# Attention into a mixture of experts on one core: gate columns beside v, merged routing steps, and a listed order

## The chip, the cores and the metric

The kernel runs on one NeuronCore of a Trainium2 chip. The core has five engines with queues of their own: TensorE (PE, with a second queue PEld for loading weights), VectorE (DVE), ScalarE (ACT), GpSimd (POOL) and SyncE (SP), and 16 DMA engines that move data between device memory and the on-chip SBUF. The metric is device microseconds (us) of one execution; shown are the median of several runs and the lowest and highest. Profiles are of one execution.

## The reference

Inputs are q, k and v of shape (8 batches, 8 heads, 576 positions, 64 channels) in float32 and three weight tables. The reference computes linear attention and then sends each token through one of eight experts:

```python
q_s = softmax(q, axis=-1)                 # over the 64 channels
k_s = softmax(k, axis=2)                  # over the 576 positions
kv  = einsum('bhsd,bhse->bhde', k_s, v)
x   = einsum('bhsd,bhde->bhse', q_s, kv)  # then (4608 tokens, 512)
logits = x @ w_gate                       # 8 experts
e      = argmax(logits)                   # one expert per token
y      = relu(x @ w1[e]) @ w2[e]          # 512 -> 1024 -> 512
out    = softmax(logits)[e] * y
```

Every softmax divides by its sum plus 1e-9.

## The kernel before, in words

The work has three parts. **Attention and routing**, one batch after another. SyncE loads k, q and v of a batch (`load`: steps LK, LQ, LV). VectorE takes the maximum of k (KM0, KM1; lines 321 to 325), TensorE turns it round (KM2, KM4), VectorE subtracts it (KS, line 357), ScalarE takes the exponential (KE), and TensorE sums k_s times v into `kv` (KV, line 375), whose first column collects the sum of k_s. ScalarE divides it into `kx` (N2), beside which the product of kv with the gate weights is put (G0 to G3). For q, VectorE finds the maximum (QM, line 441) and GpSimd subtracts it (QS, line 446). Each tile of 128 tokens is then turned round (TR), taken through ScalarE (EX), and multiplied with `kx` (MM, lines 500 and 503): 146 columns for each pair of heads, namely 128 of x, 2 sums and 16 of gate logits. VectorE adds epsilon to the sums (DE, line 508), inverts them (RE, 511), and in EV multiplies the logits into `lh` (line 515) and x into the token row `xr` (line 517). There are 36 such tiles: 4 in an even batch, 5 in an odd one.

Routing (`route`, nine times) sums the logits over the heads (LS, line 547), finds the expert of each token, counts tokens of each expert on TensorE (R5), and makes the row number in a sorted table `xs` in device memory; many small VectorE steps do this (lines 551 to 605). GpSimd then writes the token rows to `xs` with an indirect DMA for each tile (PU, line 613).

**The first expert step.** Once the first CUT batches are routed, the first 384 rows of expert 0 are loaded from `xs` (IL, line 692), turned round on TensorE (IT) and split in a high and a low part. The weights w1 of expert 0 are loaded in eight pieces through the tile `xt` (WG, line 654) and split by ScalarE (WH) and GpSimd (WL, line 662); w2 by ScalarE and VectorE (VH; VL, line 671), after the key and query tiles have given up their room (step SW). Layer 1 runs over eight blocks of the hidden width (L1, line 712, three products of four matmuls for each), then layer 2 for 128 rows (L4, line 726). A table of what the loop is to do is made from the final counts (T0 to T8), and SyncE writes rows of padding behind each expert's rows (PD, line 819).

**The expert loop** (`experts`). Each engine runs its own loop with semaphores between them. A step takes up to 384 rows of one expert. TensorE does layer 1 over 192, 256 or 384 columns (line 971), depending on how many rows the step has, and layer 2 for one, two or three tiles of 128 rows (line 987). VectorE turns the next rows round in blocks of 32 (line 1105). Ahead of the loop, TensorE finishes layer 2 of the first step (line 1013) and turns the rows of the first loop step round (line 1027).

The order of the first two parts is made by a planner: each step has an estimated cost and a due time, and `Plan.emit` puts the steps out as their turn comes. Engines work strictly in that order, and so does SyncE's queue of DMA issues. Extra matmuls into unused space (`fill`, `warm`) keep TensorE busy at places that a table names.

Of the kernel before, what the change touches and what calls it, by code (L numbers as in the profile page):

```python
# [8 lines left out]
F32 = mybir.dt.float32  # L9
# [9 lines left out]
WSTEP = 0.15  # L19
CUT = 5  # L20
# [21 lines left out]
WINDOW = 0.0
FILL = {('KM2', 1, 0): 5, ('KM2', 2, 0): 8, ('G0', 1, 0): 4, ('G0', 3, 0): 6, ('MM', 3, 2): 3, ('MM', 5, 0): 4, ('KM4', 7, 0): 8, ('G0', 6, 0): 3, ('IT', 4, 2): 4}
# [4 lines left out]
class Plan:  # L48

    LAG = {SP: 1.8, PE: 0.2, DVE: 0.2, ACTE: 0.2, POOL: 0.2}
    ISSUE, PUT, PUT_LAG = 1.4, 0.75, 1.2

    def __init__(self, bufs):
        self.bufs, self.steps = bufs, {}

    def add(self, name, b, i, eng, fn, after=(), take=None, until=(), part=1.0, at=0.0):
        self.steps[name, b, i] = SimpleNamespace(key=(name, b, i), eng=eng, fn=fn, after=[a for a in after], take=take, until=list(until),
                                                 us=COST[name] * part, rank=b + WHEN[name] + 0.02 * i, at=at)  # L60

    def start(self, a, x):
        if a.key[0] == "PU":
            return a.done
        if a.eng == x.eng:
            return a.end - a.us if x.eng == SP else a.end + 0.1 if x.eng == DVE else a.end
        return a.end + self.LAG[a.eng]

    def emit(self):
        todo = dict(self.steps)  # L70
        for x in todo.values():
            x.after = [self.steps[a] for a in x.after if a in self.steps]
            x.until = [self.steps[a] for a in x.until]
            x.end = None
        free = dict.fromkeys(self.LAG, 0.0)
        dma = 0.0
        taken = {t: [] for t in self.bufs}
        line = sorted((x for x in todo.values() if x.eng == SP), key=lambda x: x.rank)
        wait = list(todo.values())
        ready = []  # L80
        while wait or ready:
            rest = []
            for x in wait:
                (rest if any(a.end is None for a in x.after) else ready).append(x)
            wait = rest
            best = []
            for x in ready:
                if x.eng == SP and x is not line[0]:
                    continue
                t = max([free[x.eng], x.at] + [self.start(a, x) for a in x.after])  # L90
                if x.take and len(taken[x.take]) >= self.bufs[x.take]:
                    old = taken[x.take][-self.bufs[x.take]].until
                    if any(a.end is None for a in old):
                        continue
                    t = max([t] + [self.start(a, x) for a in old])
                best.append((t, x.rank, x))
            t0, _, first = min(best, key=lambda y: y[:2])
            t, _, x = min((y for y in best if y[2].eng == first.eng and y[0] <= t0 + WINDOW), key=lambda y: y[1])
            if x.eng == SP:
                line.pop(0)  # L100
                free[SP] = t
                dma = x.end = max(dma, t + self.ISSUE) + x.us
            else:
                free[x.eng] = x.end = t + x.us
            if x.key[0] == "PU":
                dma = max(dma, x.end + self.PUT_LAG) + self.PUT
                x.done = dma + self.LAG[SP]
# [7 lines left out]
def attention_moe(ctx: ExitStack, tc: tile.TileContext, q, k, v, w_gate, w1, w2, xs, out):  # L115
# [41 lines left out]
    xa_pool = xa.__enter__()  # L157
    ka = tc.tile_pool(name="ka", bufs=2, side="right")
# [103 lines left out]
    def consts():  # L262
# [8 lines left out]
        for i in range(2):  # L271
            nc.gpsimd.memset(XR[i][:, :, DM:], 0.0)
# [1011 lines left out]
```

## Time and profile before

| | |
|---|---|
| median of 3 runs | 621.72 us (615.68 to 622.42) |
| profiled execution | 612.61 us, of which 610.7 us are the span of the trace |
| PE busy | 576.1 us, 94% of the span |
| DVE busy | 328.7 us, 54% |
| ACT busy | 239.3 us, 39% |
| POOL busy | 131.6 us, 22% |
| DMA | 86.19 MB |

The span divides into three parts: attention and routing up to about 164 us, the first expert step and the passage to the loop up to 204 us, and the loop up to 605 us. A busy engine is not an engine at its peak, so the shares are read stretch by stretch.

### The profile page before, as it was taken

To read this page: it belongs to the slowest core of one execution; us is meant where nothing else is said; L and a number is where in the kernel's file an instruction comes from. 1 tells how busy PE (TensorE), PEld (TensorE's weight loads), DVE (VectorE), ACT (ScalarE), POOL (GpSimd) and SP (SyncE) were. 2 spreads that over 40 slices of the span, in tenths; PEclk is the share of its full clock that TensorE was granted. 3 is DMA by queue.
4 is the path that set the end of the run, shared out by engine and by line. 5 is a ranking of instruction groups with operands and counts; after the bars stand their busy time and mean duration, and the time that the engine had idled before them with its cause. 6 is when DMAs were issued, how large, how long until landed. Compare 5 with 4: busy or idle time off the path is not lost.

```text
span 610.7 us, 11400 instructions
## 1 busy us (share of the span) xinstructions
PE 576.1 (94%) x3811; PEld 508.0 (83%) x3812; DVE 328.7 (54%) x683; ACT 239.3 (39%) x495; POOL 131.6 (22%) x210
## 2 busy tenths in 40 slices
PE   6788968979998999999999999999999999999996
PEld 3477857767896999989898989898989999898995
DVE  6788989978870241627041413245706552662466
ACT  2557536646521221524121222225515342542453
POOL 3122555667451001020101010011010201101020
PEclk8999989989999999999999999999999999999999
DMA  9999998884754912080703020304170634145000
GB/s 256 285 263 243 304 309 228 236 249 158 261 216 143 304 30 74 0 241 8 216 17 87 17 55 31 70 34 124 72 224 17 201 122 119 52 146 178 28 21 5
DMA packets 85307, 86.19 MB, mean 141 GB/s; under 512 B 21023, under 2 KB 70687, under 8 KB 84640
## 3 DMA queue, kind: packets, MB, share of 16 engines
q1 hardware_dynamic: 79280, 66.82, 40.3%
q0 software_dynamic: 6000, 19.03, 8.4%
q8 instruction: 15, 0.25, 0.2%
q14 instruction: 12, 0.10, 0.1%
HBM read 63.88 MB, written 22.74 MB: 142 GB/s over the span
## 4 chain that ended last, share of the span: by engine, by line
PE 78%; DVE 7%; DMA 4%; issue 3%; SPq 2%; ACT 2%; POOL 2%; POOLq 0%; DVEq 0%; ACTq 0%
PE py L987 32%; PE pt L971 25%; PE ph L971 8%; PE ph L712 3%; DMA kt<-in_k 2%; PE kv L375 2%; PE xp L500 2%; DVE kp L321 1%; DVE qm L441 1%; DMA xs<-xr,posi 1%; POOL qs L446 1%; PE py L726 1%; PE py L1013 1%; ACT kx L393 1%; PE qT L487 1%
## 5 line engine op out<-in xcount | busy, mean ns | idle before, releaser
L987 PE MATMUL py<-w2h,hid 128*128 128x512 f32 x576 | 179.9, 390 | 0.0
L1117 DVE SCALAR_TENSOR_TENSOR hid<-pt,hid 128x384 fp32r<-128x384 f32 x84 | 46.4, 557 | 215.9 <-ACT hid L1052 215.6
L987 PEld LDWEIGHTS py<-w2h,hid 128*128 128x128 f32 x576 | 108.1, 188 | 22.2 <-issue 0.3
L1166 POOL DMA_INDIRECT out<-yt,ix x39 | 43.2, 1109 | 323.3 <-ACT yt L1043 323.3
L987 PE MATMUL py<-w2l,hid 128*128 128x512 f32 x288 | 112.1, 389 | 0.0
L1043 ACT ACTIVATE yt<-py,ga 128x512 f32<-128x512 f32 x39 | 26.8, 688 | 149.7 <-PE py L987 134.0
L1052 ACT ACTIVATE hid<-pt 128x384 fp32r<-128x384 f32 x84 | 41.3, 492 | 96.6 <-PE pt L971 91.5
L971 PE MATMUL pt<-xh,w1h 128*128 128x384 f32 (+2 forms) x336 | 64.9, 314 | 0.2 <-issue 0.2
L971 PE MATMUL pt<-xh,w1l 128*128 128x384 f32 (+2 forms) x336 | 64.8, 314 | 0.0
L971 PE MATMUL pt<-xl,w1h 128*128 128x384 f32 (+2 forms) x336 | 64.8, 314 | 0.0
L987 PEld LDWEIGHTS py<-w2l,hid 128*128 128x128 f32 x288 | 54.1, 188 | 10.7
L971 PEld LDWEIGHTS pt<-xh,w1h 128*128 128x128 f32 x336 | 54.7, 189 | 1.7 <-issue 0.6
L971 PEld LDWEIGHTS pt<-xl,w1h 128*128 128x128 f32 x336 | 54.3, 189 | 0.0
L971 PEld LDWEIGHTS pt<-xh,w1l 128*128 128x128 f32 x336 | 54.3, 189 | 0.0
L613 POOL DMA_INDIRECT xs<-xr,posi x36 | 36.9, 1024 | 45.7 <-DVE lh L515 23.4
L1105 DVE STREAM_TRANSPOSE xrow<-xt 128x1536 f32<-128x1536 f32 x14 | 41.3, 2951 | 3.6 <-DMA gx<-xs 3.6
L500 PE MATMUL xp<-kx,qTs 128*128 128x146 f32 x256 | 37.9, 295 | 2.9 <-DVE xr L517 1.5
L500 PEld LDWEIGHTS xp<-kx,qTs 128*128 128x128 f32 x256 | 33.9, 193 | 5.1 <-DVE xr L517 2.5
L446 POOL TENSOR_TENSOR qs<-qt,qm 128x1024 f32<-128x1024 f32 (+1 forms) x16 | 23.8, 1511 | 41.7 <-DVE qm L441 35.0
L492 ACT ACTIVATE qTs<-qT 128x512 f32<-128x512 f32 x36 | 21.2, 596 | 26.9 <-PE xp L500 15.4
L375 PE MATMUL kv<-vt,kt 128*64 128x65 f32 (+1 forms) x640 | 30.0, 236 | 0.4 <-DMA vt<-in_v 0.4
L1110 DVE TENSOR_TENSOR xl<-xrow,xh 128x1536 fp32r<-128x1536 f32 x14 | 24.6, 1757 | 10.1 <-ACT xh L1048 10.1
(207 smaller groups left out, 809.6 us busy)
## 6 DMA issues: line engine op xcount, KB each, us to landing
raw<-in_moe_w SPq DMA_DIRECT2D x10, 2048.0 KB, 8.8
vt<-in_v SPq DMA_DIRECT2D x16, 512.0 KB, 9.1
qt<-in_q SPq DMA_DIRECT2D x8, 1024.0 KB, 7.4
kt<-in_k SPq DMA_DIRECT2D x7, 1024.0 KB, 8.7
xt<-xs SPq DMA_DIRECT2D x32, 192.0 KB, 5.1
xs<-zr SPq DMA_DIRECT2D x11, 260.0 KB, 2.4
xt<-in_moe_w SPq DMA_DIRECT2D x8, 256.0 KB, 5.5
raw<-in_moe_w SPq DMA_DIRECT2D x4, 512.0 KB, 6.1
```

The costliest lines, as they stand in the source:

```text
L375: nc.tensor.matmul(o.kv[i * D:(i + 1) * D, c, lo:lo + D + 1], o.kt[:r, 2 * c + i, j, :], VT[b % 2][:r, 2 * c + i, at:at + D + 1], start=Fa ...
L446: nc.gpsimd.tensor_tensor(o.qs[:, j0:j1].rearrange("p j h d -> p h j d"), o.qt[:, :, j0:j1, :], o.qm[:, :, j0:j1, None].to_broadcast([P, H ...
L500: nc.tensor.matmul(xv[:, c, :KW], o.qT[i][:, c, :], kx[:, c, :], start=True, stop=True)
L613: s = nc.gpsimd.indirect_dma_start(out=xs, out_offset=bass.IndirectOffsetOnAxis(ap=n.pi[:, t - t0:t - t0 + 1], axis=0), in_=xr[:, t, :], i ...
L971: m = e.matmul(ph, wt[:, c, f * P:(f + 1) * P], xt[:, c, :w], start=(n == 0), stop=(n == 3 * NC - 1))
L987: m = e.matmul(g.PY[u], ht[:, f, u * P:(u + 1) * P], wt[:, f, :], start=(n == 0), stop=(n == 3 * NF - 1))
L1043: m = e.activation(g.YT[u], g.PY[u], AF.Copy, scale=g.GA[:, u:u + 1]).wait_op(sPY[u], cu[u], GE)
L1052: e.activation(g.HH[:, f, :], g.PH[f][:, :W], AF.Relu).wait_op(sPH[f], it, GE).then_inc(sHH[f], 1)
L1105: e.transpose(g.XR.rearrange("p c (k j) -> p k c j", j=32), xblocks(g.XT).rearrange("p k (l c) -> p k c l", c=NC)).wait_op(sX, ld, GE).the ...
L1110: e.tensor_tensor(v(g.XL), src, v(g.XH).bitcast(F32), op=ALU.subtract).wait_op(sXH, it, GE).then_inc(sXL, 1)
L1117: e.scalar_tensor_tensor(g.HL[:, f, :], g.PH[f][:, :W], 0.0, g.HH[:, f, :].bitcast(F32), op0=ALU.max, op1=ALU.subtract).wait_op(sHH[f], it ...
L1166: e.indirect_dma_start(out=g.out, out_offset=bass.IndirectOffsetOnAxis(ap=g.IX[:, u:u + 1], axis=0), in_=g.YT[u], in_offset=None, bounds_c ...
```

## The change

- **Columns of `kx`.** A pair of heads has its 146 columns as 8 gate, 64 x, 64 x, 8 gate, then the 2 sums. One VectorE multiply then writes x and logits together into the token row, which grows from 520 to 584 floats, and LS reads the logits out of that row.
- **Merged steps.** Epsilon is put into `kv` by the matmul that clears it; the running count is a column of the one-hot tile; the expert's base row is added on TensorE; epsilon of the gate softmax is a constant column; the last sum writes the integer position itself. Five kinds of small VectorE steps go.
- **Order.** The planner's costs are replaced by a list of all steps, each with its number of fills. The q tile has two buffers. Expert 0's w1 comes in two loads into a tile of its own, and the first expert step's rows come from the first 4 batches instead of 5.
- **First loop step.** Its rows are loaded in blocks and turned round by VectorE as in every other step, and SyncE reads the two table entries for that load before the loop's code starts.
- **Narrow layer 1.** The narrow form has 224 columns instead of 192, and the threshold for taking it is raised to 224 rows.

```diff
-CUT = 5
+CUT = 4
-COST = dict(VG=1.5, VH=1.0, VL=1.2, LK=3.3, LV=4.0, LQ=3.3, CD=1.1, CS=1.31, KM0=2.2, KM1=0.7, KM2=0.45, KM3=0.6, KM4=0.95,
...
+ORDER = """
+CD.0.0.0 LK.0.0.0 LK.0.1.0 LK.0.2.0 LK.1.0.0 KM0.0.0.0 LK.1.1.0 LQ.0.0.0 LV.0.0.0 KM0.0.1.0 KM1.0.0.0 KM2.0.0.47 KM3.0.0.0
...
-                o.qt = ka_pool.tile([P, H, FULL, D], F32, name="qt", bufs=1)
+                o.qt = ka_pool.tile([P, H, FULL, D], F32, name="qt", bufs=2)
...
-            nc.tensor.matmul(t, none16[:1].to_broadcast([1, P]), none16[:1, :, None].to_broadcast([1, NP, D + 2]), **flags)
+            nc.tensor.matmul(t, ones16[:65], eps16[:65], **flags)
...
-            TS(ks, ks, EPS, None, op0=ALU.add)
             nc.vector.reciprocal(o.kr, ks)
...
         def ev(i):
             xv, qd = o.xp[i], o.qd[i]
-            TT(o.lh[:, i].rearrange("p (c i) e -> p c i e", i=2), xv[:, :, 2 * D + 2:KW].rearrange("p c (i e) -> p c i e", i=2),
-               qd[:, :, :, None].to_broadcast([P, NP, 2, E]), op=ALU.mult)
-            TT(xr[:, i, :DM].rearrange("p (c i d) -> p c i d", c=NP, i=2), xv[:, :, :2 * D].rearrange("p c (i d) -> p c i d", i=2),
-               qd[:, :, :, None].to_broadcast([P, NP, 2, D]), op=ALU.mult)
+            TT(xr[:, i, :XW].rearrange("p (c i d) -> p c i d", c=NP, i=2), xv[:, :, :KG].rearrange("p c (i d) -> p c i d", i=2),
+               qd[:, :, :, None].to_broadcast([P, NP, 2, D + E]), op=ALU.mult)
...
         def lsum():
-            RED(lg, o.lh[:, sl].rearrange("p t h e -> p t e h"), op=ALU.add, axis=AX.X)
+            g = xr[:, sl, :XW].rearrange("p t (c x e) -> p t e c x", c=NP, e=E)[:, :, :, :, 0:KG // E:KG // E - 1]
+            RED(lg, g, op=ALU.add, axis=AX.XY)
...
-        def a7():
-            acc[b, t1] = cst.tile([P, E], BF, name=f"acc{b}_{t1}", tag="acc", bufs=3)
-            TT(acc[b, t1], acc[prev], sm, op=ALU.add)
-        def a8():
-            n.cm = small("cm")
-            TS(n.cm[:, :T], cm, float(-RS), float(E * RS), op0=ALU.mult, op1=ALU.add)
-        def a12():
-            TS(se, se, EPS, None, op0=ALU.add)
-        def a13():
-            TT(n.pi[:, :T], pos, n.cm[:, :T], op=ALU.add)
...
+    def w1_get(g):
+        f = slice(g * FW, (g + 1) * FW)
+        nc.sync.dma_start(I0.RAW1[:, :, f], w1[0].rearrange("(p c) f -> p c f", c=NC)[:, :, f])
...
-                    layer1(P + P // 2)
+                    layer1(2 * P - P // 4)
...
-        e.wait_ge(sX, 3 * 16)
-        for u in (2, 1, 0):
-            for c in range(NC):
-                m = e.transpose(g.PT[:, u, c, :], xcol(g.XT, u, c, DM), g.ident)
-        m.then_inc(sT, 1)
         first(2)
...
-        evac(lambda t: t.rearrange("p c (u t) -> p u c t", t=P), g.PT, g.XT[:, :, DM:DM + 2])
+        turn_x()
+        evac()
...
-        n = x.get(KD, 0, 0, 6)
-        row = x.get(ROW, 0, 0, E * RS)
-        for u in range(3):
-            with e.If(n > 2 * u):
-                e.dma_start(g.XT[:, u, :], g.xs[bass.ds(row + u * P, P), :]).then_inc(sX, 16)
+        rows(*g.AT0)
```

The list moves instructions at three places that matter below. First, the start of SyncE's queue. Before (`kt`, `vt`, `qt` are the key, value and query tiles, `in_` the inputs):

```order
L190 DMA kt<-in_k 128x4x256 x2
L192 DMA kt<-in_k 64x8x64
L190 DMA kt<-in_k 128x8x256
L192 DMA kt<-in_k 64x8x64
L196 DMA vt_90<-in_v 128x8x128 [waits Pool_49]
L204 DMA qt<-in_q 128x8x256
```

Now (`wg` are the gate weights, `zr` a tile of padding that GpSimd fills):

```order
L308 DMA wg<-in_moe_w_gate 64x4x8 [waits Pool_49]
L308 DMA wg<-in_moe_w_gate 64x4x8
L311 DMA xs<-zr 128x584 [waits Pool_49]
L311 DMA xs<-zr 128x584 x2
L206 DMA kt<-in_k 128x4x256 x2
L208 DMA kt<-in_k 64x8x64
```

The gate weights and the three writes of padding, which came ninth and later, now stand ahead of the first key load, and wait for GpSimd.

Second, GpSimd's queue at the split of expert 0's w1 (`w1l` is the low part of w1, `xs<-xr` the write of a tile of token rows, `xr_119` and `xr_120` the rows of an even and of an odd batch). Before, with the sixth batch's query rows `qs` ahead:

```order
L446 TENSOR_TENSOR qs<-qt,qm 128x512
L455 TENSOR_TENSOR qsr<-qr,qmr 128x512
L662 TENSOR_TENSOR w1l_62<-xt,w1h_61 128x512 x3
L609 COPY xr_115<-tok 128x5
L612 MEMSET spacer 1x1
L613 DMA xs<-xr_115,posi 42624x520
L662 TENSOR_TENSOR w1l_62<-xt,w1h_61 128x512 x2
```

Now:

```order
L667 TENSOR_TENSOR w1l_62<-raw_73,w1h_61 128x512 x3
L619 COPY xr_119<-tok 128x4
L667 TENSOR_TENSOR w1l_62<-raw_73,w1h_61 128x512
L622 MEMSET spacer 1x1
L623 DMA xs<-xr_119,posi 43776x584
```

The split stood among the writes of the fourth and fifth batches; now it stands behind the writes of the sixth, four pieces ahead of the seventh batch's four writes and four ahead of the eighth's.

Third, TensorE at the end of layer 1 of the first step (`ph` is a layer-1 block, `xp` the last token tile, `cn` the final count from which the table and the padding rows are made). Before, the last token tiles ran ahead of all of layer 1, and five blocks came behind the count:

```order
L712 MATMUL ph_2315<-xh,w1l_62 128x384 x4
L758 LDWEIGHTS ones_107
L758 MATMUL cn<-acc_5_2344,ones_107 128x8
L712 MATMUL ph_2352<-xh,w1h_61 128x384 x4
L712 MATMUL ph_2352<-xl,w1h_61 128x384 x4
```

Now:

```order
L521 MATMUL xp<-kx_99,qTs 128x146 x4
L713 MATMUL ph_2246<-xh,w1h_61 128x384 x4
L713 MATMUL ph_2246<-xl,w1h_61 128x384 x4
L713 MATMUL ph_2246<-xh,w1l_62 128x384 x4
L713 MATMUL ph_2271<-xh,w1h_61 128x384 x4
L713 MATMUL ph_2271<-xl,w1h_61 128x384 x4
L713 MATMUL ph_2271<-xh,w1l_62 128x384 x4
L759 LDWEIGHTS ones_109
L759 MATMUL cn<-oh_138,ones_109 128x8
L713 MATMUL ph_2295<-xh,w1h_61 128x384 x4
```

Four blocks of layer 1 stand ahead of the last token tile, and two blocks behind the count.

## Rows read from the trace of the kernel before

**Rows 1.** Windows by stage: length, busy (instructions) per engine, granted clock, DMA share, GB/s
```profile
0.00:44.00 44.00, 34.30 (x307) 22.95 (x308) 31.04 (x67) 19.50 (x48) 12.49 (x51) 0.96 1.07 266
44.00:107.00 63.00, 52.35 (x559) 43.93 (x559) 57.15 (x163) 36.60 (x107) 28.09 (x39) 0.95 1.03 272
107.00:164.00 57.00, 50.85 (x550) 42.27 (x546) 49.91 (x163) 33.60 (x88) 36.13 (x53) 0.97 0.75 232
164.00:182.00 18.00, 17.92 (x108) 16.81 (x109) 15.02 (x70) 6.50 (x12) 9.04 (x16) 1.00 0.52 198
182.00:204.00 22.00, 19.68 (x91) 15.47 (x91) 3.00 (x9) 3.94 (x5) 1.99 (x2) 1.00 0.59 207
204.00:605.00 401.00, 400.96 (x2207) 366.52 (x2205) 172.56 (x214) 138.44 (x236) 42.89 (x50) 1.00 0.30 90
```

**Rows 2.** Timeline of SyncE's queue: start us, duration us, line and operation
```profile
0.78 1.01 SPq L190 DMA_DIRECT2D kt<-in_k  x2
...
143.75 1.30 SPq L692 DMA_DIRECT2D xt<-xs  x3
...
173.44 9.08 SPq L819 DMA_DIRECT2D xs<-zr  x8
190.73 2.03 SPq L1241 DMA_DIRECT2D xt<-xs  x3
```

**Rows 3.** Timeline of GpSimd: the padding tile, and a write of token rows
```profile
6.12 0.14 POOL L140 IOTA zr<- 128x1 f32 x1
...
151.43 0.97 POOL L613 DMA_INDIRECT xs<-xr,posi  x1 [0.23 <-issue]
```

**Rows 4.** Timeline of VectorE: two small routing steps, a tile's multiplies
```profile
74.23 0.16 DVE L586 TENSOR_SCALAR cm<-own 128x5 f32<-128x5 f32 x1
74.35 0.17 DVE L599 TENSOR_SCALAR own<-own 128x5 f32<-128x5 f32 x1
...
151.40 0.22 DVE L515 TENSOR_TENSOR lh<-xp,qden 128x64 f32<-128x64 f32 x1
151.54 0.68 DVE L517 TENSOR_TENSOR xr<-xp,qden 128x512 f32<-128x512 f32 x1
```

**Rows 5.** Timeline of VectorE: two long instructions, and the first when undisturbed
```profile
81.16 3.98 DVE L321 TENSOR_TENSOR kp<-kt 128x512 f32<-128x512 f32 x1
...
85.63 0.69 DVE L321 TENSOR_TENSOR kp<-kt 128x512 f32<-128x512 f32 x1
...
116.65 2.93 DVE L322 TENSOR_TENSOR km<-kp 128x256 f32<-128x256 f32 x1
```

**Rows 6.** Timeline of GpSimd beside the first of these
```profile
81.64 2.93 POOL L446 TENSOR_TENSOR qs<-qt,qm 128x1024 f32<-128x1024 f32 x2
```

**Rows 7.** Groups by line and form: count, busy us, mean ns, idle before
```profile
L1105 DVE STREAM_TRANSPOSE xrow<-xt 128x1536 f32<-128x1536 f32 x14 | 41.3, 2951 | 3.6 <-DMA gx<-xs 3.6
L662 POOL TENSOR_TENSOR w1l<-xt,w1h 128x512 fp32r<-128x512 f32 x8 | 10.0, 1272 | 0.5 <-ACT w1h L658 0.4
L671 DVE TENSOR_TENSOR w2l<-raw,w2h 128x1024 fp32r<-128x1024 f32 x4 | 4.9, 1214 | 0.0
L547 DVE TENSOR_REDUCE own<-lh 128x32 f32<-128x256 f32 x4 | 2.4, 608 | 0.0
```

**Rows 8.** Chain that ended last, in order of time: start us, length us, engine, line
```profile
126.54 2.31 PE mb L176 x8
...
182.24 5.72 PE py L726 x24
...
196.15 1.72 PE pt L1027 x12
...
214.18 6.24 PE pt L971 x36
...
401.62 4.00 PE pt L971 x36
...
456.22 4.32 PE pt L971 x36
```

More of the change, by code (lines that the diff above doesn't have):

```diff
@@ L48 @@
 class Plan:
-    LAG = {SP: 1.8, PE: 0.2, DVE: 0.2, ACTE: 0.2, POOL: 0.2}
-    ISSUE, PUT, PUT_LAG = 1.4, 0.75, 1.2
     def __init__(self, bufs):
[L56 to L76, printed above, removed]
-        taken = {t: [] for t in self.bufs}
[L78 to L107, printed above, removed]
@@ new lines, in __init__, with add, emit @@
+        self.bufs, self.steps, self.fills = bufs, {}, {}
+    def add(self, name, b, i, eng, fn, after=(), take=None, until=()):
+        self.steps[name, b, i] = SimpleNamespace(eng=eng, fn=fn, after=list(after), take=take, until=list(until))
+    def emit(self, order):
+        queue = []
+        for word in order.split():
+            name, b, i, n = word.split(".")
+            key = (name, int(b), int(i))
+            queue.append(key)
+            self.fills[key] = int(n)
+        assert sorted(queue) == sorted(self.steps)
+        seen = set()
+        taken = {t: [] for t in self.bufs}
+        for key in queue:
+            x = self.steps[key]
+            assert all(a in seen for a in x.after if a in self.steps), key
@@ L108, in emit @@
             if x.take:
+                if len(taken[x.take]) >= self.bufs[x.take]:
+                    assert all(a in seen for a in taken[x.take][-self.bufs[x.take]].until), key
                 taken[x.take].append(x)
-            ready.remove(x)
+            seen.add(key)
             x.fn()
@@ L622, in route @@
         old = [("PU", b - 2, t) for t in range(t0, t1)]
[L623 removed]
+        add("LS", b, r, DVE, lsum, [("EV", b, t) for t in range(t0, t1)])
         add("R0", b, r, DVE, a0, [("LS", b, r)])
@@ L684, in first_count @@
         I0.cn = ps.tile([P, E], F32, name="cn", tag="sm", bufs=1)
-        nc.tensor.matmul(I0.cn, ones16, acc[last5], start=True, stop=True)
+        nc.tensor.matmul(I0.cn, ones16, OH[turn[last5]][:, 0], start=True, stop=True)
     def first_rows():
@@ L757, in t0 @@
             n.cn = ps.tile([P, E], F32, name="cn", tag="sm", bufs=1)
-            nc.tensor.matmul(n.cn, ones16, acc[B - 1, SLOT], start=True, stop=True)
+            nc.tensor.matmul(n.cn, ones16, OH[turn[B - 1, SLOT]][:, 0], start=True, stop=True)
         def t1():
@@ L877, in attention_moe @@
     tables()
-    for n in range(WARM):
-        add("WM", 0, n, PE, lambda n=n: warm(n), at=WARM0 + n * WARMD, take=None if n else "xp", until=[("WM", 0, WARM - 1)])
-    plan.emit()
+    plan.emit(ORDER)
     nc.gpsimd.memset(spacer, 0.0)
```

302 lines of the change are left out of this document (174 added, 128 removed).

## The prediction, made before the changed kernel ran

> **What bounds the kernel now.** I read the windows by stage first [rows 1]. In the loop, 204 to 605 us, TensorE is busy 400.96 of 401 us: there only a shorter or missing matmul helps. From 164 to 182 us TensorE is busy 17.92 of 18 us with the eight layer-1 blocks of the first expert step, 2.24 us each. Attention and routing, 0 to 164 us, have no such single owner. Up to 107 us the DMA share is above 1.0, so the loads queue behind each other; VectorE is busy 31.04 of the first 44 us, then 57.15 of 63 (91%) and 49.91 of 57 (88%). From 107 us the DMA share is 0.75. So the loads set the pace at the start, VectorE nearly sets it from 44 us, and what is left is 5.9 and 7.1 us in which VectorE waits, plus time in which it is held up while it counts as busy: one maximum over keys took 3.98 us, its like 0.69, and another instruction of that step 2.93 [rows 5].
>
> Last I read the chain [rows 8] for what the stages hand on: layer 2 of the first step (5.72 us), twelve transposes between it and the loop (1.72 us), and the loop's layer 1 by width.
>
> **The change part by part.**
>
> *The start.* The first key load is issued at 0.78 us [rows 2]. Behind the listed order it stands after three writes of the padding tile, whose last value GpSimd writes at 6.12 + 0.14 = 6.26 us [rows 3]. SyncE's queue is in order, so all key, value and query loads behind wait too, and with them everything. The bytes of the padding and the gate weights are moved today as well, only later in the same full queue; what is lost is the time with no load under way, 6.26 - 0.78 = **+5.5 us**. Ends: 0, if VectorE's slack of 13 us in the first 44 us swallows it, and +7, with the issue of the three writes. I take 5.5, because the DMA engines have no slack in that stage.
>
> *Fewer VectorE instructions.* The logits' multiply disappears 36 times; the next instruction starts 0.14 us after it [rows 4], so it is worth 5.0 us. The multiply into the token row grows from 512 to 576 elements: 0.68 us x 64/512 = 0.085, 36 times, 3.1 us back. Five kinds of small steps go: epsilon of kv 8 times, the running count, the base row, epsilon of the gate softmax and the last add 9 times each, 44 in all, at one step per 0.12 us [rows 4]: 5.3 us. Together -7.2 us. VectorE is 90% busy where they stand, so I count nine tenths, **-6.5 us**. Ends: -7.2, and 0 if the loads set the pace throughout. The sum of logits now reads a strided row; four tiles take 0.608 us today [rows 7], nine such sums 5.5 us; that they double is the far end, that they stay the same is what I take, since today's read is strided already. The new additive matmuls on TensorE lie beside VectorE's work.
>
> *The waits.* The list places one wait after another differently, and no row shows the result. Nothing back is one end. The other is all 13 us of VectorE's waits from 44 to 164 us and the 3.3 + 2.5 us of the held-up instructions, -19. Some of it must go: the eight fills ahead of the last batch's subtraction, 2.31 us on the chain [rows 8], are not in the list, w1's eight loads no longer stand between key, value and query loads, and a second q tile lets a load go out a batch earlier. But a wait that goes often uncovers the next. I take a quarter, **-5 us**.
>
> *Token rows* grow by 256 bytes: 4608 x 256 = 1.2 MB, 4.3 us of DMA at 272 GB/s [rows 1]. At a share of 0.75 from 107 us on this is covered; uncovered it costs those 4.3.
>
> *First expert step and passage.* The twelve transposes leave TensorE (1.72), and VectorE's turning takes 2.95 us [rows 7] while TensorE has the third tile of layer 2 to do, some 5.7 us. SyncE has the two table entries in hand, and its three row loads (2.03 us) become five. Against that, the final count now stands two blocks from the end of layer 1 instead of five. Behind the count, SyncE issues the eight padding writes for 9.08 us [rows 2]; TensorE has 2 x 2.24 + 5.72 = 10.2 us left, and the passage waits for the writes to land. Today they are issued by 182.5 and layer 2 ends at 188.0, which leaves 5.4 us. So up to 2 us are gained and up to 2.5 lost: **0**.
>
> *Narrow layer 1.* Thirty-six matmuls take 6.24 us at 384 columns, 4.32 at 256, 4.00 at 192 [rows 8]: 0.173, 0.120, 0.111 us each. From 384 to 256 that is 0.42 ns for each column; the same line gives 0.107 at 224 and 0.093 at 192, but 192 shows 0.111, so a floor is reached before, and 224 should cost that floor. The reference's inputs leave two last steps of 211 and 194 rows, which go from 256 to 224, and three of 158, 173 and 34, which go from 192 to 224. Each step has 96 such matmuls: 2 x 96 x 0.009 = **-1.7 us**; on a straight line between 192 and 256 it would be +0.4.
>
> Sum: 5.5 - 6.5 - 5 + 0 - 1.7 = -7.7. The profiled execution took 612.61 us (a span of 610.7), 1.5% less than the median of 621.72; it would come to 604.9. The same 7.7 us off the median give 614.0, and I predict **614 us**.
>
> **The rivals.**
>
> *No change: the loads set the pace.* For it: the DMA share above 1.0 to 107 us [rows 1]. Then what VectorE saves turns into waiting, and the start's 5.5 us and the wider rows of the first four batches (18 tiles, 0.6 MB, 2.2 us) stand against w1's 2.1 MB, which no longer run ahead of the last loads (7.7 us at 272 GB/s): 0, and with the loop's -1.7, 620. Against it: VectorE at 91% while the queue is full.
>
> *Slower: GpSimd's queue in the end of attention.* The first step's rows are read behind the last value load, then w1 is loaded, and GpSimd must do nine writes, four low parts, four writes and four low parts before the fifth layer-1 block may start. A write takes 0.09 + 0.97 + 0.23, some 1.28 us with its pause [rows 3], a low part 1.27 [rows 7]: 13 x 1.28 + 8 x 1.27 = 26.8 us. Four blocks add 9.0 us. Layer 2 starts at 182.2 today, so the rows must land by 146.4 us; today they are issued at 143.75 [rows 2]. With the start 5.5 us later they could land at 153, and layer 2 starts at 188.8: +6.6, with 2.5 from the padding and -1.7 from the loop +7.4, 629. It decides from a landing at 146.4 us on, and costs over 1% from 152. Against it: the read no longer waits for the fifth batch's writes, which held it today.
>
> *VectorE and GpSimd hold each other up at the end.* The 3.98 us began while GpSimd was at the query subtraction, which read SBUF from 81.64 for 2.93 us [rows 5, 6]; VectorE's instruction has both its inputs in SBUF and ended at 85.14, 0.6 us after that one. The low parts of w1 stand now beside the four low parts of w2 on VectorE, 1.21 us each [rows 7], of the same kind, in a stretch where VectorE is busy 15.02 of 18 us. If each is held for one low part of w1, 4 x 1.27 = 5.1 us come back to VectorE, and to the hidden rows for which layer 1 waits: -2.6, 619. Against it: the list puts writes between the low parts, and a layer-1 block leaves 2.24 us for VectorE's 0.55. The Trainium skill, SBUF — State Buffer, "Who interferes with whom", says that a VectorE instruction with two SBUF inputs and a GpSimd instruction that reads SBUF take a shared read interface in turn, and that the later one is blocked for the whole of the other. The trace agrees, with the 3.98 us.
>
> *A denser order.* Half the waits go instead of a quarter: another -5, 609; at its best 604. For it: behind the third batch's keys the list has 17 fills where the planner's table had 32, as if it left TensorE fewer gaps.
>
> *The change doesn't do what it says*: the narrow form is not taken, or the wide multiply costs as much as the two. -1.7 or -1.9 are missing: 616.
>
> **How the numbers follow.** A difference of 1%, 6.2 us, is about what a measurement here can tell from none; the three runs shown lie 6.7 us apart. Chances: the forecast 0.45, of which 0.35 lies more than 1% below; denser order 0.12; no change 0.20; holding up 0.08; GpSimd's queue 0.13; not as said 0.02. Faster 0.35 + 0.12 = 0.47; the same 0.10 + 0.20 + 0.08 + 0.02 = 0.40; slower 0.13. The likeliest case alone, with the bounds of start, passage and waits, is 610 to 618. Nearly half the chance is on other cases: from 605, nearly the best of the denser order, to 625, which leaves out most of the slower case and no more.
>
> **What would show it.** In the changed profile: the first key load at 6.3 us or later; VectorE with some 7 us less work in front of layer 1 and no separate logits multiply; its waits between 44 us and layer 1 below 13 us; the first layer-2 block of the first step at about 175 us; no width of 192 or 256 in the loop but five of 224 at 4.0 us for 36 matmuls. I am wrong if the last batch's loads land when they do today and the rest only follows; if GpSimd is busy without a pause up to the fifth layer-1 block; or if the late start is made up within the first batches, which would make the gain larger by 5 us.

## The result: slower by 1.4%, and the profile after

The changed kernel takes 627.14 us (four runs, 625.18 to 628.25), the kernel before, beside it, 620.47 (615.68 to 622.42): a ratio of 1.0136, 95% interval 1.0087 to 1.0185. Forecast were 614 us (605 to 625) and a gain. The profiled execution took 627.72 us, of which 625.9 are its span.

The windows of the changed kernel by stage (length; busy us and instructions of TensorE, its weight loads, VectorE, ScalarE, GpSimd; granted clock, DMA share, GB/s), to be read against [rows 1]:

```profile
0.00:44.00 44.00, 34.23 (x219) 18.93 (x221) 25.82 (x56) 13.81 (x34) 10.82 (x53) 0.92 0.95 234
44.00:107.00 63.00, 54.34 (x612) 46.33 (x612) 52.74 (x132) 36.83 (x109) 27.74 (x39) 0.92 1.10 285
107.00:168.20 61.20, 55.83 (x586) 48.74 (x584) 46.06 (x134) 37.13 (x100) 29.78 (x47) 0.92 0.75 232
168.20:195.40 27.20, 21.78 (x119) 19.94 (x120) 21.88 (x65) 7.38 (x14) 12.59 (x20) 0.87 0.30 116
195.40:218.30 22.90, 17.22 (x79) 13.54 (x77) 5.99 (x13) 3.44 (x4) 4.48 (x7) 1.00 0.84 256
218.30:621.00 402.70, 401.89 (x2208) 367.13 (x2208) 172.51 (x215) 138.98 (x236) 43.12 (x50) 1.00 0.31 90
```

The loop is about as long as before (402.7 and 401 us). Layer 1 of the first expert step, 18 us with TensorE busy throughout, now lasts 27.2 with TensorE busy 21.78 at a granted clock of 0.87. VectorE is busy 124.6 us ahead of that stage and waits 43.6.

SyncE's queue (start, duration, line and operation), against [rows 2]: the first key load goes out at 7.74 us instead of 0.78, the first step's rows earlier than before, the padding writes 18 us later.

```profile
6.33 1.37 SPq L311 DMA_DIRECT2D xs<-zr  x3
7.74 1.39 SPq L206 DMA_DIRECT2D kt<-in_k  x2
...
130.49 1.47 SPq L690 DMA_DIRECT2D xt<-xs  x3
...
191.32 8.20 SPq L823 DMA_DIRECT2D xs<-zr  x8
...
206.51 0.40 SPq L914 DMA_DIRECT2D gx<-xs  x1
```

The groups by line and form (count, busy us, mean ns, idle before), against [rows 7]: the wide multiply, the loop's turning, and the low parts of w1 and w2. Those of w2 took 1.214 us each and take 2.589.

```profile
L1102 DVE STREAM_TRANSPOSE xrow<-xt 128x1536 f32<-128x1536 f32 x15 | 44.1, 2941 | 17.5 <-DMA gx<-xs 17.5
L536 DVE TENSOR_TENSOR xr<-xp,qden 128x576 f32<-128x576 f32 x36 | 27.1, 753 | 0.6
L676 DVE TENSOR_TENSOR w2l<-raw,w2h 128x1024 fp32r<-128x1024 f32 x4 | 10.3, 2589 | 0.0
L667 POOL TENSOR_TENSOR w1l<-raw,w1h 128x512 fp32r<-128x512 f32 x8 | 10.0, 1277 | 0.0
```

The mean hides that three of the four are as before and one is not. VectorE's timeline in layer 1 (start, duration):

```profile
172.05 0.55 DVE L720 SCALAR_TENSOR_TENSOR hid<-ph,hid 128x384 fp32r<-128x384 f32 x1
172.52 6.70 DVE L676 TENSOR_TENSOR w2l<-raw,w2h 128x1024 fp32r<-128x1024 f32 x1
...
179.23 0.54 DVE L720 SCALAR_TENSOR_TENSOR hid<-ph,hid 128x384 fp32r<-128x384 f32 x1
```

GpSimd's there:

```profile
172.05 0.97 POOL L623 DMA_INDIRECT xs<-xr,posi  x1 [0.23 <-issue]
173.05 3.75 POOL L667 TENSOR_TENSOR w1l<-raw,w1h 128x512 fp32r<-128x512 f32 x3
176.74 0.18 POOL L619 COPY xr<-tok 128x3 f32<-128x3 f32 x1
176.88 1.25 POOL L667 TENSOR_TENSOR w1l<-raw,w1h 128x512 fp32r<-128x512 f32 x1
```

And TensorE's, with two windows around it:

```profile
174.15 0.86 PE L713 MATMUL ph<-xh,w1l 128*128 128x384 f32 x4
179.83 1.65 PE L713 MATMUL ph<-xh,w1h 128*128 128x384 f32 x4 [4.82 <-DVE hid L720]
181.28 1.48 PE L713 MATMUL ph<-xl,w1h 128*128 128x384 f32 x4
```

```profile
175.00:180.00 5.00, 0.18 (x2) 0.17 (x2) 5.00 (x4) 0.49 (x1) 3.17 (x5) 0.80 0.00 0
180.00:185.00 5.00, 5.00 (x22) 4.69 (x23) 2.57 (x9) 0.49 (x1) 0.00 (x0) 0.52 0.01 3
```

One low part of w2 lasts 6.70 us: from 0.53 us before GpSimd's row of low parts to 1.09 us after its end. The hidden rows `hid` (line 720) stand behind it in VectorE's order, TensorE waits 4.82 us for them, and then runs some 5 us at 0.52, its lower clock of 1.2 GHz: four matmuls take 1.48 us that took 0.86.

The chain of waits (start, length), against [rows 8]: a wait for extra matmuls at the start, the slow block, the last piece of the first loop rows, their turning, and layer 1 at 384 and at 224 columns.

```profile
28.06 3.66 PE mb L191 x9
...
179.83 4.21 PE ph L713 x12
...
206.51 5.49 DMA gx<-xs
212.03 2.92 DVE xrow L1102
```

```profile
218.30 8.08 PE pt L973 x36
...
418.27 4.01 PE pt L973 x36
422.28 2.68 PE ph L973 x24
424.96 4.02 PE pt L973 x36
```

**Chips.** The runs below came from several chips. On one of them the kernel before takes 620 us, on the three others 612 to 613; so only ratios to the kernel before beside it are compared. By its times the profile above is from the slower kind; that of [rows 1] was not shown to be. Executions of one kernel on one chip also differ in the granted clock: of ten of e8 below, four took 606.0 to 608.1 us at a mean of 0.988 to 0.991, six 612.6 to 614.1 at 0.973 to 0.977. Both kernels were profiled again on one chip, and these two profiles give the account. TensorE's rows of the kernel before (layer 1, layer 2, first loop step):

```profile
162.32 0.95 PE L712 MATMUL ph<-xh,w1h 128*128 128x384 f32 x4 [0.21 <-DVE pe L555]
180.41 0.50 PE L726 MATMUL py<-w2h,hid 128*128 128x512 f32 x1
```

```profile
201.88 6.50 PE pt L971 x36
```

Of the changed kernel:

```profile
156.85 0.94 PE L713 MATMUL ph<-xh,w1h 128*128 128x384 f32 x4 [0.18 <-DVE xr L536]
183.87 0.47 PE L727 MATMUL py<-w2h,hid 128*128 128x512 f32 x1
```

```profile
207.12 8.06 PE pt L973 x36
```

In us, from the start of the one row to the start of the next:

| stage | before | changed | difference |
|---|---|---|---|
| to layer 1 of the first step | 162.32 | 156.85 | -5.5 |
| layer 1 | 18.09 | 27.02 | +8.9 |
| layer 2 to the loop | 21.47 | 23.25 | +1.8 |
| first 36 matmuls of the loop | 6.50 | 8.06 | +1.6 |
| the rest of the loop | 400.7 | 399.6 | -1.1 |
| span | 609.1 | 614.8 | +5.7 |

### The profile page after: what moved, and what is told of

Its sections match the earlier page's. It is cut to its first block, busy times and chain, and to the rows that moved or that the text cites. A ratio compares the mean times of both kernels' runs of the same rounds, so it can differ in the third digit from the quotient of the medians.

```text
span 625.9 us, 11354 instructions
## 1 busy us (share of the span) xinstructions
PE 585.3 (94%) x3813; PEld 514.6 (82%) x3814; DVE 325.0 (52%) x610; ACT 237.6 (38%) x495; POOL 129.5 (21%) x213
## 4 chain that ended last, share of the span: by engine, by line
PE 77%; DVE 10%; issue 3%; ACT 3%; DMA 3%; SPq 2%; another core or an unknown queue 1%; POOL 1%; POOLq 0%; DVEq 0%; ACTq 0%
PE py L989 31%; PE pt L973 25%; PE ph L973 8%; PE xp L521 3%; PE kv L402 3%; DVE kt L383 2%; PE qT L508 1%; DVE xr L536 1%; PE ph L713 1%; DMA kt<-in_k 1%; DVE kp L347 1%; DMA gx<-xs 1%; ACT kx L419 1%; DVE qm L464 1%
## 5 line engine op out<-in xcount | busy, mean ns | idle before, releaser
L973 PE MATMUL pt<-xh,w1h 128*128 128x384 f32 (+1 forms) x336 | 65.0, 315 | 3.2 <-DVE xl L1107 3.2
L973 PE MATMUL pt<-xl,w1h 128*128 128x384 f32 (+1 forms) x336 | 65.0, 315 | 0.0
L973 PE MATMUL pt<-xh,w1l 128*128 128x384 f32 (+1 forms) x336 | 65.0, 315 | 0.0
L1102 DVE STREAM_TRANSPOSE xrow<-xt 128x1536 f32<-128x1536 f32 x15 | 44.1, 2941 | 17.5 <-DMA gx<-xs 17.5
L623 POOL DMA_INDIRECT xs<-xr,posi x36 | 35.6, 988 | 50.2 <-DVE kp L347 10.4
L521 PE MATMUL xp<-kx,qTs 128*128 128x146 f32 x256 | 40.7, 308 | 0.4 <-DVE ge L579 0.3
L521 PEld LDWEIGHTS xp<-kx,qTs 128*128 128x128 f32 x256 | 37.0, 207 | 1.2 <-issue 0.9
L402 PE MATMUL kv<-vt,kt 128*64 128x65 f32 (+1 forms) x640 | 32.0, 237 | 1.6 <-issue 1.6
L402 PEld LDWEIGHTS kv<-vt,kt 128*64 128x64 f32 (+1 forms) x640 | 25.7, 141 | 8.7 <-issue 4.7
L1107 DVE TENSOR_TENSOR xl<-xrow,xh 128x1536 fp32r<-128x1536 f32 x15 | 26.4, 1760 | 11.6 <-ACT xh L1045 11.6
```

Source lines behind the costliest of these rows:

```text
L402: nc.tensor.matmul(o.kv[i * D:(i + 1) * D, c, lo:lo + D + 1], o.kt[:r, 2 * c + i, j, :], VT[b % 2][:r, 2 * c + i, at:at + D + 1], start=Fa ...
L521: nc.tensor.matmul(xv[:, c, :KW], o.qT[i][:, c, :], kx[:, c, :], start=True, stop=True)
L623: s = nc.gpsimd.indirect_dma_start(out=xs, out_offset=bass.IndirectOffsetOnAxis(ap=n.pi[:, t - t0:t - t0 + 1], axis=0), in_=xr[:, t, :], i ...
L973: m = e.matmul(ph, wt[:, c, f * P:(f + 1) * P], xt[:, c, :w], start=(n == 0), stop=(n == 3 * NC - 1))
L1102: e.transpose(g.XR.rearrange("p c (k j) -> p k c j", j=32), xblocks(g.XT).rearrange("p k (l c) -> p k c l", c=NC)).wait_op(sX, ld, GE).the ...
L1107: e.tensor_tensor(g.XL, g.XR, g.XH.bitcast(F32), op=ALU.subtract).wait_op(sXH, it, GE).then_inc(sXL, 1)
```

## The experiments

**The changed kernel again** (c1, c2), beside other kernels on two chips, and the kernel before once more (b1).

> The changed kernel as it is, beside the kernel before on the same chip as the kernels it is compared with. If what the first comparison showed belongs to the kernel, its time is again 1.3% above the kernel before, and the profile again shows two unexplained stops of ScalarE of 3 to 4 us and a sum of keys times values of 7.6 us instead of 3.6. If those stops belonged to that execution, layer 1 starts at 162 instead of 168.2, as it does in the kernel with only w2's low parts moved, and the ratio is 1.008 to 1.012.

> The changed kernel as it is, once more beside the kernels of this group: 1.010 to 1.014 times the kernel before on either chip, with layer 2 of the first step starting at about 189 us where the stops are missing and at 195 to 197 where they are not.

> The kernel before as it is, for one more profile of it, from the chip on which the other kernels of this group run. If the pieces into which the third sum of keys times values falls (7.6 us instead of 3.6) and ScalarE's stop of 3 to 4 us come with that chip, the kernel before shows stops of this kind there too, and its own 8 us between the two chips (612 and 620) lie in them. If they belong to the changed kernel's order, the kernel before shows none.

Ratios 1.0117 (1.0051 to 1.0183) and 1.0123 (1.0081 to 1.0166): the loss belongs to the kernel, not to the chip. The stops do go with the chip. In the profile after and in the four from the slower chip (the changed kernel again, e5, e6, e7), the fifth batch's sum of keys times values falls into pieces and takes 7.8 to 9.2 us; in the profiles from the other chips it is one piece of 3.6 us. The kernel before splits that sum by its own order, with a wait for VectorE between, so its profiles say nothing on this. TensorE's rows from the profile after:

```profile
94.43 0.34 PE L402 MATMUL kv<-vt,kt 128*64 128x65 f32 x3 [0.43 <-issue]
95.14 0.37 PE L402 MATMUL kv<-vt,kt 128*64 128x65 f32 x4 [0.37 <-issue]
95.88 1.73 PE L402 MATMUL kv<-vt,kt 128*64 128x65 f32 x9 [0.38 <-issue]
```

There layer 1 of the changed kernel starts at 168.24 and 169.67 us, elsewhere at 156.85. The kernel before loses 8 us on that chip too; where, no profile shows.

**The start** (e1): `CD`, the gate weights and the three padding writes, moved behind the first value load.

```diff
-CD.0.0.0 LK.0.0.0 ... LV.0.0.0
+LK.0.0.0 ... LV.0.0.0 CD.0.0.0
```

> The changed kernel (627 us) with the gate weights and the three padding writes issued behind the first value load instead of ahead of the first key load. If the late start is carried through to the end, the first key maximum comes at about 6.4 us instead of 15.1, the first block of layer 1 moves from 168.2 to about 161 to 163, and the time falls by 5 to 8 us, to 619 to 622. If the 43 us in which VectorE waits ahead of layer 1 swallow it, the first block stays within 2 us of 168 and the time within 2 us of 627. If it is the order behind that paces, something between.

Ratio 1.0045 (1.0011 to 1.0078), about 0.8% below the changed kernel. The keys land 8 us earlier, but layer 1 starts at 154.77, 2.1 earlier than in the changed kernel's profile c2. Between them stand 47 extra matmuls that the list has ahead of the first turning. TensorE's row and VectorE's:

```profile
2.16 12.81 PE L191 MATMUL kmT<-ones 128*128 128x512 bf16 x47 [2.16 <-DVE ones L255]
```

```profile
15.45 0.69 DVE L361 TENSOR_REDUCE mx<-kmT 128x4 f32<-128x512 f32 x1 [7.15 <-PE kmT L357]
```

Of the three forecasts the last fits, something between: most of the 8 us is waited for again. The profiles of e1 and c2 have the same mean clock, 0.985, and spans of 613.0 and 614.8 us, so at a like clock some 2 us are gained; the 0.8% compares medians of executions at different clocks.

**Low parts of w2 later** (e2), **both edits** (e3).

```diff
-VL.7.0.0 L1.3.1.0 PU.6.2.0 L2.3.0.0 VL.7.1.0 ... VL.7.2.0 L1.3.2.0 WL.0.4.0 ... VL.7.3.0
+L3.3.2.0 VL.7.0.0 ... L3.3.3.0 VL.7.1.0 VL.7.2.0 ... L3.3.4.0 VL.7.3.0
```

> The changed kernel with only the four low parts of w2 on VectorE moved behind the last low part of w1 on GpSimd. If it is the two engines' sharing of SBUF that stretched one low part of w2 from 1.2 to 6.7 us and let TensorE stop for 4.8 us and then run at half its clock, all four take 1.2 us, the pause between the third and the fourth block goes, the clock stays at full, and layer 2 starts 7 to 9 us earlier (187 instead of 195.4): 618 to 620. If the hidden rows wait for something else, for example the routing steps or GpSimd itself, layer 2 starts no earlier than 193 and the time stays at 625 to 627.

> Both of these edits together. If the two costs are independent they add up: 13 to 16 us off 627, thus 611 to 614. If the earlier start only runs into the same later wait, the gain is that of the second edit alone, 618 to 620.

e2: 1.0052 (1.0015 to 1.0089); layer 2 starts at 185.9, and layer 1 lasts 23.9 us instead of 27. The pause of 4.8 us is gone, one of 2.6 is left: the first moved part meets the end of GpSimd's row and takes 3.47 us. e3: 0.9998 (0.9970 to 1.0026), so the two gains nearly add up, and together they are as large as the loss. Against the kernel before there is no gain.

**The count early** (e4): the last token tile and both routing parts among the first blocks, the count behind the fourth block, and all of w1's low parts in a row ahead of the writes.

```diff
-VL.7.1.0 ... L1.3.2.0 WL.0.4.0 ... L1.3.5.0 ... T0.7.0.0
+MM.7.4.0 ... L1.3.0.0 VH.7.0.0 WL.0.4.0 WL.0.5.0 WL.0.6.0 WL.0.7.0 PU.6.0.0 ... L1.3.3.0 ... T0.7.0.0
```

> The early loads, and behind them the order of the end: the last token tile and both of the last batch's routing parts ahead of or among the first blocks of layer 1, the final count four blocks from the end of layer 1 instead of two, the eight padding writes that much earlier, and w1's low parts all ahead of the sixth batch's writes, w2's behind them. If the passage waits for the padding writes to land, TensorE no longer waits 2.4 us behind layer 2, the rows of the first loop step land 4 to 5 us earlier relative to layer 2, and from the start of layer 2 to the start of the loop it is 18 to 19 us instead of 22.9: 607 to 610. If the row load itself is what takes the time (5.5 us for the last piece, beside the weights), the passage stays at 21 to 23 us and the time is that of the run with both edits.

A miss: 1.0050 (1.0021 to 1.0079). The passage, from layer 2 to the loop, is 21.8 us: 2 less than in e3, but not the 18 to 19 expected, since the rows still take 6 us to land. And the row of eight low parts held another VectorE instruction, of 32 columns, which began in the third of them. VectorE's row and GpSimd's:

```profile
149.24 7.42 DVE L576 TENSOR_TENSOR pb<-own,lm 128x32 f32<-128x32 f32 x1
```

```profile
150.33 0.18 POOL L619 COPY xr<-tok 128x4 f32<-128x4 f32 x1
150.47 6.13 POOL L667 TENSOR_TENSOR w1l<-raw,w1h 128x512 fp32r<-128x512 f32 x5
```

An instruction that takes some 0.17 us undisturbed lasted through six low parts and a copy, to the end of the row, and layer 1 started at 163.25 instead of 154.6.

**Low parts apart** (e5, from e4; e10, from the changed kernel alone). The edit of e10:

```diff
-PU.6.0.0 ... PU.6.3.0 ... WL.0.4.0 WL.0.5.0 WL.0.6.0 WL.0.7.0
+PU.6.0.0 WL.0.4.0 PU.6.1.0 WL.0.5.0 PU.6.2.0 WL.0.6.0 PU.6.3.0 WL.0.7.0
```

> The order of the run with the early count, with w1's low parts on GpSimd one by one between the token writes of the sixth and seventh batches instead of in rows of three and five. If a VectorE instruction with two inputs in SBUF is held until GpSimd's whole row of low parts is through, the difference of the logits and their maximum takes at most 1.4 us instead of 7.4, the first block of layer 1 starts at 156 to 157 instead of 163.3, and the time falls by 5 to 7 us against the run with the early count: ratio 0.993 to 0.996 to the kernel before. If a token write does not let VectorE in either, or layer 1 waits for the low parts' later end, the time stays at 1.003 to 1.005.

> The changed kernel with one edit: the second four low parts of w1 on GpSimd one by one behind the four writes of the seventh batch, instead of four in a row; w2's low parts on VectorE stay where they are. If a VectorE instruction with two inputs in SBUF is held until a whole row of GpSimd's low parts is through, and a write between them lets it in, the third low part of w2 takes at most 2.6 us instead of 6.7, TensorE stops for less than 2 us instead of 4.8, layer 2 starts 4 to 6 us earlier, and the ratio is 1.002 to 1.006 instead of 1.012. If what counts is that both run in the same stretch, however they are mixed, the four low parts of w2 together stay at 10 us or more and the ratio at 1.010 or more.

e10 decides what holds VectorE: with nothing in GpSimd's queue moved but the four low parts, the third low part of w2 takes 1.21 us instead of 6.70, and all four 7.05 together, not 10.3. The ratio is 1.0067 (1.0038 to 1.0095) instead of 1.012. VectorE's row there and GpSimd's:

```profile
159.61 2.96 DVE L676 TENSOR_TENSOR w2l<-raw,w2h 128x1024 fp32r<-128x1024 f32 x1
```

```profile
160.19 1.29 POOL L667 TENSOR_TENSOR w1l<-raw,w1h 128x512 fp32r<-128x512 f32 x1
161.41 0.09 POOL L622 MEMSET spacer<- 1x1 f32 x1
161.67 1.76 POOL L623 DMA_INDIRECT xs<-xr,posi  x1 [0.17 <-issue]
```

A low part that begins 0.58 us before GpSimd's ends 1.09 us after it, as in the profile after, but now after one, since a spacer and a write follow instead of another low part. The size is a miss: two of the four low parts and two small instructions are still held, TensorE stops for 3.23 us, not under 2, and layer 1 lasts 25.9 us where it was 27.0. So of the 3.5 us by which the span is shorter than c2's only 1.1 lie in layer 1; the rest, in the passage and the loop's first matmuls, is not traced to the hold. e5, where a small instruction still takes 2.83 us behind a row of two, has 1.0019 (0.9975 to 1.0062): less gain than expected, on the slower chip, where e4 did not run.

These profiles also say when a hold begins. In e8 below, VectorE's row and GpSimd's:

```profile
154.45 2.84 DVE L579 SCALAR_TENSOR_TENSOR ge<-pb,dec 128x32 f32<-128x32 f32 x1
```

```profile
153.71 0.99 POOL L623 DMA_INDIRECT xs<-xr,posi  x1 [0.17 <-issue]
154.74 2.50 POOL L667 TENSOR_TENSOR w1l<-raw,w1h 128x512 fp32r<-128x512 f32 x2
```

This instruction takes 0.18 us undisturbed and begins 0.28 us ahead of the low parts' row; it is held all the same. Over all profiles, ahead of the loop, each VectorE instruction with two SBUF inputs that began in a token write, up to 0.57 us ahead of a low part or a query subtraction following directly on it, was held, and none that began 0.77 us ahead or earlier. Where GpSimd had stood idle, 0.21 us were enough: line 325 of the kernel before takes 0.63 us there, as elsewhere. So the later start of GpSimd's row does not show that VectorE came first.

**The passage** (e6 from e3, e8 from e5): three loads of 128 whole rows and one for the gates, twelve transposes on TensorE between layer 2's tiles, as before.

```diff
-        rows(*g.AT0)
+            for t in range(u):
+                e.dma_start(g.XT[:, t, :]...).then_inc(sX, 16)
...
+        e.wait_ge(sX, LOADS)
+        for u in (2, 1, 0):
+            for c in range(NC):
+                m = e.transpose(g.PT[:, u, c, :], xcol(g.XT, u, c, DM), g.ident)
```

> Both edits (early loads, w2's low parts later), and the first loop step's rows loaded tile by tile and turned round by twelve transposes on TensorE between layer 2's second and third tile, as in the kernel before. If the block load and VectorE's turning are what the passage pays, it is 2 to 4 us shorter from the start of layer 2 to the start of the loop (20 to 21.5 instead of 23.7 us), and the ratio to the kernel before is 0.994 to 0.997 instead of 1.000. If the late padding writes alone pay, the passage stays within 1 us of 23.7.

> The run with w1's low parts apart, with the first loop step's rows loaded tile by tile and turned by TensorE. There the padding writes are early enough, so that only the row load is left: from the start of layer 2 to the start of the loop 19 to 20 us instead of 21.5, ratio to the kernel before 0.997 to 1.000 where the run with the low parts apart had 1.002. If TensorE stands between layer 2's tiles for the rows, it stays at 21 us or more.

e6: 1.0005 (0.9972 to 1.0039), passage 23.2 us, nothing gained: TensorE waits for SyncE's padding writes first. e8, with the writes earlier: 20.9 us, and 0.9969 (0.9934 to 1.0003). The two limits stand behind one another; each edit alone takes 0 to 2 us off the passage.

**Two multiplies** (e7 from the changed kernel; e12 from e11).

```diff
+            TT(gates(xo), gates(xv[:, :, :KG]), qd[:, :, :, None].to_broadcast([P, NP, 2, E]), op=ALU.mult)
```

> The changed kernel with the wide multiply taken apart again: one for the 64 logits and one for the 512 columns of x, 36 tiles, all else as in the changed kernel. By the prediction's term 36 x (0.14 - 0.085) = 2 us of VectorE come back, nine tenths of them on the path: 1.8 us slower than the changed kernel. If VectorE does not set the pace of attention, as its 43 us of waits ahead of layer 1 say, the time stays within 1 us of the changed kernel.

> The same with the wide multiply taken apart into one for the 64 logits and one for the 512 columns of x. In the changed kernel itself this cost nothing. If VectorE paces attention once the late start, the fills and the holds are gone, 2 us come back, ratio 0.003 above the run beside it; if it still waits, the two are within 0.001.

e7: 1.0122 (1.0056 to 1.0187) beside 1.0117. e12: 0.9976 (0.9947 to 1.0006) beside 1.0003. The 36 instructions come back in both, and the time doesn't, as far as this can be told: 0.003 was forecast, which e7's interval is too wide to see; e12 came out 0.003 lower, not higher.

**Fewer extra matmuls** (e9 from e8), **and the rest** (e11 from e9).

```diff
-KM2.0.0.47 ... KM4.1.0.9
+KM2.0.0.20 ... KM4.1.0.2
```

> The same with 20 instead of 47 extra matmuls ahead of the first turning of the key maxima, and 2 instead of 9 ahead of the second batch's subtraction. The 47 were listed for keys that land at 15 us; with keys at 6.4 us they hold up the first subtraction by some 6 us (VectorE waits 6.8 us for the turning), the 9 by 2 to 3. If the path goes through them, the first block of layer 1 starts 6 to 9 us earlier than in the run without this edit, and the ratio falls by 0.010 to 0.014, to 0.985 to 0.990: better than both kernels. If the loads set the pace there, or the clock falls for want of work, less than 3 us come.

> The run with fewer extra matmuls, with the last row of two low parts broken up as well, the first low part ahead of the sixth batch's writes, and the first block of layer 1 ahead of the last token tile. If what is left are the holds of 2.8 and 1.7 us and the tile ahead of layer 1, the first block starts at 153 to 155 instead of 157.4 and the ratio is 0.988 to 0.991. If layer 1 is paced by the routing of the last batch, it ends as late as there, and the ratio stays at 0.993 to 0.995.

e9: 0.9941 (0.9903 to 0.9979), below both kernels, but only 0.003 below e8, with intervals that overlap. The executions at the higher clock take 606.9 to 609.4 us in e9 (six of ten, 0.980 to 0.985) and 606.0 to 608.1 in e8 (four of ten), so no gain of this edit by itself is shown. In the profiles layer 1 starts 6.1 us earlier than in e8 (157.43, 163.49) and layer 2 5.9. Only 3.3 us of that stand ahead of the seventh batch's sum of keys times values: in e8's profile the granted clock is 0.50 there, and the sum takes 5.96 us instead of 3.58. Then TensorE stands for 3.4 us ahead of the loop, and the first 36 matmuls take 8.97 us where they took 6.30. That gives the gain back in e9's profile:

```profile
194.14 5.49 PE py L1015 x24
199.63 3.43 issue
203.06 8.97 PE pt L973 x36
```

e11: 1.0003 (0.9978 to 1.0028), a miss: layer 1 starts at 154.17 as expected, layer 2 at 179.06, no earlier than in e9, and the pause is 4.1 us; in e12 it is 3.6. e8 has none. In the three pauses the split rows (`xl`) are ready 5.6 us or more before TensorE goes on, and the profile names no releaser. A packet of 16 KB of a queue that carries instructions ends in each of them, 1.70 to 1.72 us before the loop's first matmul; in e8 it ends 1.84 us before. That TensorE waits there for its own code would fit, and no run tests it.

## Why the prediction was wrong

- **First expert step: 0 was wrong, +8.9.** This is the step that failed. The clash was among the rivals, with a chance of 0.08 and a price of 5.1 us. The mechanism was right and both numbers were not. The price assumed one low part of GpSimd for each of VectorE; the trace and e10 show an instruction held for the whole unbroken row. The prediction's own rows had this: it says that the instruction of 3.98 us began while GpSimd was at the subtraction, but by [rows 5, 6] it began 0.48 us ahead of a row of two subtractions and ended 0.57 us after both. The reason against it, that the list puts writes between the low parts, was wrong by its own order rows: the first four are shown there in a row (three, a copy, one), and the second four stand the same way behind the writes. And the price left out what follows a hold. Of the 8.9 us, 4.8 are the pause, 2.0 the block at the lower clock (4.2 instead of 2.2), and 1.2 the last tile, which now runs inside layer 1.
- The Trainium skill, SBUF — State Buffer, "Who interferes with whom", says that the order of issue decides which of the two engines blocks the other. By the rows the low part of w2 began first, 0.53 us ahead, and was held for all four; but as e8's rows show, the start of GpSimd's row is not where its hold begins, so the trace does not decide against the rule. That VectorE's instruction, already waiting, was passed by three more low parts is what the trace adds.
- **The start: +5.5.** The keys came 8 us later, as the mechanism says, and VectorE waits 6.6 us more in the first 44 us than in the kernel before. But taking the late start away gives only 2.1 us at layer 1 with the 47 matmuls in place (e1); without them 3.3 more are shown (e8, e9).
- **Fewer VectorE instructions: -6.5.** They went: VectorE is busy 127.8 us ahead of layer 1 where it was 138.1, on one chip. Some 4.8 of these 10.3 us are time in which instructions were held beyond what their like take (9.4 us before, 4.5 now), which the prediction counted under the waits. Putting the 36 back, 2 of the 7.2 us, cost nothing measurable (e7, e12): a share of 90% was read as a path. The 44 small steps were not put back.
- **The waits: -5.** The sum of start, instructions and waits was -6.0, and layer 1 starts 5.5 us earlier on the chip with both profiles. VectorE's waits from 44 us to layer 1 fell only from 11.9 to 10.2 us there; with the 4.8 us of holds that is -6.5. That the sum fits does not show what each part is worth in time.
- **The passage: 0, with -2 to +2.5.** +1.8, and +1.6 behind it: the loop's first 36 matmuls run after a pause, 8.06 instead of 6.50 us. The padding writes decide it, as foreseen, and behind them the rows' last piece, 5.3 to 6.0 us from issue to landing, and VectorE's turning, which the prediction set off against fewer transposes.
- **Narrow layer 1: -1.7 was right.** 224 columns take 4.01 us for 36 matmuls, as 192 did. Two steps go from 11.52 to 10.71 us: -1.6.
- **Token rows: 0**, not tested by itself.
- **GpSimd's queue**, the slower rival, did not decide: the load of the first step's rows was issued at 130.49 us, long before its limit of 146.4, and GpSimd stood idle for VectorE for 4.6 and 3.4 us among its last writes. The forecast had slower at 0.13, on the wrong mechanism.

## What to carry to other kernels

Where GpSimd and VectorE both combine two SBUF tiles, look at the order on GpSimd's queue, not at its busy share: put other work, as here a spacer and a token write, between its long instructions, and keep VectorE's instructions with two SBUF inputs out of the stretch when TensorE waits behind them. A late start and the filling made for it belong together: change one, and the other becomes the wait. A term for fewer instructions on a 90% busy engine needs a row that shows work waiting for that engine, else it is only assumed.

## What the runs showed that was not expected

- VectorE's instruction with two SBUF inputs was held through a whole row of GpSimd's: 6.70 us in five profiles (the changed kernel three times, e1, e7), 7.42 us for 32 columns in e4, behind six low parts and a copy. The hold began up to 0.57 us ahead of the row's start in the profile. A token write with a spacer behind it does not hold VectorE: two low parts of w2 took 2.36 us beside two such writes in the profile after. A write that begins while such a low part runs is itself slowed: 1.76 instead of 0.97 us in e10.
- After a pause of 4.8 us the granted clock was 0.52 for some 5 us. In e8's and e2's profiles it was 0.50 through the seventh sum of keys times values, with no pause in that sum; why is open.
- One of four chips takes 8 us longer with the kernel before, and stops TensorE inside one and the same sum in the four profiles from there, as in the profile after; the cause is open.
